# Moving four shares of y and their copy-out within the first quarter of each token group, in a fused attention and two-MLP kernel

## The chip, the cores and the metric

The kernel runs on one core of one Trainium2 chip. The metric is the device time of one execution, in microseconds (us), from launch to end, as the median of several runs. One further execution was recorded by the hardware profiler; all rows below come from it.

## What is computed

A pooled attention is followed by two MLPs without biases; the change touches the second MLP alone.

```python
def _moe2_ref(x, w_in, w_out):            # x: 4608 x 512
    h = x @ w_in                          # w_in: 512 x 2048
    relu6 = np.clip(h + 3.0, 0.0, 6.0)
    g = h * relu6 / 6.0
    return (g @ w_out).astype(np.float32) # w_out: 2048 x 512

def reference(...):
    attn_out = _attn_ref(q, k, v)         # softmax attention on keys and values pooled by 8
    x = attn_out, heads side by side      # 4608 x 512
    x = _moe_ref(x, w_in, w_out)          # as above, with g = h * sigmoid(h)
    return _moe2_ref(x, ...)
```

All of it is float32. A matrix product is made of three TensorE products of rounded parts (high by high, low by high, high by low), which is why most operands come in pairs such as `gh` and `gl`.

## The kernel before

**Staging.** The whole body stands in a manual schedule: each engine runs its instructions in the order in which the program issues them. A first stage (up to about 915 us of the span) does the attention and the first MLP and writes its result to the DRAM tensors `x1`. The second MLP is the loop at lines 851 to 918: `g` runs over 9 groups of 512 tokens, and inside it `d` runs over 4 quarters of the hidden units (512 units each, four blocks `f` of 128).

**A quarter.** The product with `w_in` is done by a seven-product block scheme: `product(bank, g, d, k)` (line 588) issues 12 matmuls of half width, and k is one of 0, 5, 4, 6, 3, 1, 2 in this order. Below they are P0, P5, P4, P6, P3, P1, P2. P0, P4 and P1 take turns on the two PSUM buffers of pool `ps_h`, the other four on the two of `ps_a`. A buffer is free again when VectorE (DVE) or ScalarE (ACT) has read it: `c1` is an ACT copy of P0 (line 878), and `add` (line 862) is a DVE addition that makes u2 = c1 + P5, then u3 = u2 + P6, u4 = u3 + P4, u2 = u2 + P4, later u3 + P3, c1 + P1 and u2 + P2. So P3 needs the buffer that the first addition frees, and P6 of the next quarter needs the one that the last addition frees.

**Activations.** `act_half` (line 609) is called four times in a quarter, for u4, u3, c1 and u2, in this order: an ACT relu (line 612), a DVE min-and-multiply (line 613), an ACT copy to the rounded high part `gh` (line 620), a DVE subtraction for the low part `gl` (line 621). Each of the four needs the one before. The first two calls fill `gh2` and `gl2`, from which blocks 1 and 3 of the quarter are read; the last two fill `gh1` and `gl1`, for blocks 0 and 2. ACT and DVE thus run one chain, and between two calls DVE does the next addition.

**Shares of y.** The product with `w_out` is added up over the 16 blocks of a group in four PSUM banks (pool `ps_y`, one buffer each). A share is one block's part: `y_mm` (line 508) issues 12 matmuls, three for each bank, with `gh` or `gl` as the weights. Shares wait in the list `todo`; `y_next` (line 844) issues the oldest. A quarter calls it four times: after P5, after the three additions behind P6, after the third `act_half`, and after the fourth. The shares of a quarter are thus issued in the next one; those of the last quarter (blocks 13, 15, 12, 14) come in the first quarter (d = 0) of the next group. Behind block 14 comes `y_out` (line 527): four copies out of the banks, two on ACT (line 532) and two on DVE (line 534), and four DMA issues on SyncE's queue (line 541). The next group's first share overwrites the banks, and so needs these copies.

**Other work of a quarter.** `passed(k)` issues on SyncE's queue the load of the next weights of product k (line 232). In the second quarter `load_x1` issues loads of the next group's x; in the third and fourth, `made` has GpSimd (POOL, lines 178 and 585) and ACT (line 584) make its seven block operands.

Of the kernel before, what the change touches and what calls it, by code (L numbers as in the profile page):

```python
# [25 lines left out]
def kernel(  # L26
# [54 lines left out]
    def shuffled(ap):  # L81
        return ap.rearrange("p (a n) -> p n a", a=2)
# [136 lines left out]
    def load_split(f):  # L219
        t = wts.tile([P, 2, DM], F32R, tag=f"o{f}", name="whl")  # L220
        nc.sync.dma_start(out=t.bitcast(F32), in_=w2[f])
        w_sl[1, f, 1] = (t[:, 0], t[:, 1])
# [6 lines left out]
    def load_factor(d, k):  # L229
        i = PASSING.index(k) if k in PASSING else 4 + 3 * d + STAYING.index(k)  # L230
        t = wts.tile([P, 2, 2, HW], F32R, tag=f"i{i}", name="wst")
        nc.sync.dma_start(out=t.bitcast(F32), in_=ws[d][k])
        w_st[d, k] = t
# [274 lines left out]
    def y_mm(layer, g, f):  # L508
        gh, gl = g_t.pop((layer, g, f))
        oh, ol = w_sl[layer, f, 1]  # L510
        if f == FIRST[layer]:
            y_ps[layer, g] = [
                ps_y.tile([P, 512], F32, tag=f"y{i}", name=f"y{i}") for i in range(4)
            ]
        for i, ps in enumerate(y_ps[layer, g]):
            sl = slice(i * P, (i + 1) * P)
            if layer == 0:
                prods = ((oh[:, sl], gh), (ol[:, sl], gh), (oh[:, sl], gl))
            else:
                prods = ((gh[:, sl], oh), (gh[:, sl], ol), (gl[:, sl], oh))  # L520
            for n, (a, b) in enumerate(prods):
                nc.tensor.matmul(  # L522
                    ps, a, shuffled(b), start=(f == FIRST[layer] and n == 0),
                    stop=(f == LAST[layer] and n == 2),
                )

    def y_out(layer, g):
        scale = 0.5 if layer == 0 else 1.0 / 6.0
        for i, ps in enumerate(y_ps.pop((layer, g))):
            o = p2.tile([P, 512], F32, tag="o", name="o", bufs=4)  # L530
            if i % 2 == 0:
                nc.scalar.activation(in_two(o), dealt(ps), AF.Copy, scale=scale)  # L532
            else:
                nc.vector.tensor_scalar(
                    out=in_two(o), in0=dealt(ps), scalar1=scale, scalar2=None, op0=ALU.mult
                )
            if layer == 0:
                dst = x1[g][i * P:(i + 1) * P, :]
            else:
                dst = out[g * GT + i * P:g * GT + (i + 1) * P, :]  # L540
            nc.sync.dma_start(out=dst, in_=o)
# [12 lines left out]
    def open_rest():  # L554

        four = p2.tile([P, 4, 2, GT], F32R, tag="x", name="xst")
        late["x"] += [four[:, i] for i in range(4)]

    def load_x1(g):

        for k in range(2):
            for n in range(2):
                r = late["pool"].tile([P, 2, HW], F32, tag="r", name="xr", bufs=4)
                rows = x1[g][k * HW:(k + 1) * HW, n * HW:(n + 1) * HW]
                nc.sync.dma_start(out=r, in_=rows.rearrange("(c p) t -> p c t", p=P))
                x_raw[k, n] = r.rearrange("p c t -> p (c t)")
# [3 lines left out]
    def make_x(g, i):  # L570

        k = MADE[i]
        b11, b12, b21, b22 = (x_raw[a, b] for a in range(2) for b in range(2))
        src = (b11, b11, b11, b12, b21, b21, b22)[i]
        if i == 1:
            combine(ALU.subtract, b11, b12, b11)
        elif i == 2:
            combine(ALU.subtract, b11, b22, b11)
        elif i == 3:
            combine(ALU.subtract, b12, b22, b12)  # L580
        elif i == 5:
            combine(ALU.subtract, b21, b21, b11)
        t = late["x"][(7 * g + i) % 9]
        nc.scalar.activation(t[:, 0], src, AF.Copy)  # L584
        nc.gpsimd.tensor_tensor(out=t[:, 1], in0=src, in1=t[:, 0].bitcast(F32), op=ALU.subtract)  # L585
        x_st[g, k] = t.rearrange("p a (c n) -> p a c n", c=2)

    def product(bank, g, d, k):

        pool, tag = bank  # L590
        ps = pool.tile([P, GT], F32, tag=tag, name=f"p{k}")
        w = w_st[d, k].rearrange("p j a (c f) -> p j a c f", f=P)
        x = x_st[g, k]
        for j in range(2):
            for n, (a, b) in enumerate(((0, 0), (1, 0), (0, 1))):
                for c in range(2):
                    nc.tensor.matmul(  # L597
                        ps[:, j * HW:(j + 1) * HW],
                        w[:, j, a, c, :],
                        shuffled(x[:, b, c, :]),  # L600
                        start=(j == 0 and n == 0 and c == 0),
                        stop=(j == 1 and n == 2 and c == 1),
                    )
        return ps

    def rows_of(name, bufs):
        return late["pool"].tile([P, 2, GT], F32R, tag=name, name=name, bufs=bufs)
# [44 lines left out]
    with tc.manual_schedule():  # L652
# [191 lines left out]
        def y_next():  # L844
            if todo:
                l, g, f = todo.pop(0)
                y_mm(l, g, f)
                if f == LAST[l]:
                    y_out(l, g)

        for g in range(NG):
            for d in range(NF // 4):
                more = g + 1 < NG
                nd = (d + 1) % (NF // 4)
                go = more or d + 1 < NF // 4
                c1 = p2.tile([P, GT], F32, tag="gh", name="c1")
                u2 = p2.tile([P, GT], F32, tag="gl", name="u2")
                u3 = late["pool"].tile([P, GT], F32, tag="u3", name="u3")
                u4 = late["pool"].tile([P, GT], F32, tag="u4", name="u4", bufs=1)

                def add(out, a, b):
                    nc.vector.tensor_tensor(out=out, in0=a, in1=b, op=ALU.add)  # L862

                def passed(k):
                    if go:
                        load_factor(nd, k)

                def made(*items):
                    for i in items:
                        make_x(g + 1, i)  # L870

                if g == 0 and d == 0:
                    open_rest()
                    make_x(0, 5)
                    make_x(0, 6)
                p1 = product((ps_h, "h"), g, d, 0)
                passed(0)
                nc.scalar.activation(c1, p1, AF.Copy)
                add(u2, c1, product((ps_a, "a"), g, d, 5))
                y_next()  # L880
                if g == 0 and d == 0:
                    load_split(NF - 1)
                if more and d == 1:
                    load_x1(g + 1)
                if more and d == 2:
                    made(0)
                p5 = product((ps_h, "h"), g, d, 4)
                passed(4)
                add(u3, u2, product((ps_a, "a"), g, d, 6))
                add(u4, u3, p5)  # L890
                add(u2, u2, p5)
                y_next()
                gh2, gl2 = rows_of("gh2", 1), rows_of("gl2", 1)
                act_half(u4, 1, gh2, gl2)
                if more and d == 2:
                    made(1)
                if more and d == 3:
                    made(2, 3)
                add(u3, u3, product((ps_a, "a"), g, d, 3))
                act_half(u3, 0, gh2, gl2)  # L900
                add(c1, c1, product((ps_h, "h"), g, d, 1))
                passed(1)
                gh1, gl1 = rows_of("gh1", 2), rows_of("gl1", 2)
                act_half(c1, 0, gh1, gl1)
                y_next()
                if more and d == 3:
                    made(4, 5)
                add(u2, u2, product((ps_a, "a"), g, d, 2))
                passed(2)
                act_half(u2, 1, gh1, gl1)  # L910
                y_next()
                if more and d == 3:
                    made(6)
                for f, gh, gl, j in ((1, gh2, gl2, 0), (3, gh2, gl2, 1), (0, gh1, gl1, 0), (2, gh1, gl1, 1)):
                    g_t[1, g, 4 * d + f] = (gh[:, j], gl[:, j])
                    todo.append((1, g, 4 * d + f))
# [50 lines left out]
```

## Time and profile before

| what | us |
|---|---|
| median of 3 runs (1687.97 to 1690.34) | 1690.16 |
| the profiled execution, device time | 1689.02 |
| its span, first to last instruction | 1687.2 |
| TensorE busy, share of the span | 95% |
| VectorE, ScalarE, GpSimd busy | 61%, 37%, 23% |

A row of the timeline gives start, duration, engine, line, operation, output and inputs, how many instructions are merged, and in brackets the idle time of the engine before it with what ended it. PE is TensorE's matmuls, PEld its weight loads. Times are us from the span's start. A row of the windows view gives for a stretch its length, the busy time of each engine with its instructions, the granted TensorE clock (1.00 is the full 2.4 GHz), the DMA share and the rate.

### The profile page before, as it was taken

The page shows a single profiled execution, that of the slowest core. Times are in us where ns is not written, and L with a number is a line of the kernel's source. Part 1 is how long each engine was busy: PE and PEld are TensorE (multiplying, and loading weights), DVE is VectorE, ACT ScalarE, POOL GpSimd, SP SyncE. Part 2 cuts the span into 40 slices and gives each one's busy share as a digit, 9 for nine tenths or more (in the row PEclk, how much of TensorE's full clock was granted, in tenths as well). Part 3 has the DMA queues.
Part 4 walks back from the last instruction along what each step waited for, and adds up shares of the span by engine and source line. Part 5 has one row for each costly group of instructions (what it writes and reads, how often), then busy time and mean ns, then how long its engine had stood idle before and what let it go on. Part 6 is the DMA issues. An engine that isn't in the chain of part 4 may idle for free.

```text
span 1687.2 us, 24141 instructions
## 1 busy us (share of the span) xinstructions
PE 1602.4 (95%) x9312; PEld 1419.0 (84%) x9312; DVE 1031.0 (61%) x1608; ACT 631.8 (37%) x1094; POOL 381.8 (23%) x377
## 2 busy tenths in 40 slices
PE   7787999999999999999999999999999999999999
PEld 6566888888888888888889898989898989898988
DVE  6999767677676777665423655555555555555554
ACT  5454433333343333333322433333333333333333
POOL 4755322222312132211021121212121212020200
PEclk9798999999999999999999999999999999999999
DMA  9251334344443445432356434343434343434341
GB/s 284 103 198 32 106 124 154 109 152 155 136 152 106 149 149 161 131 131 83 108 203 237 150 100 142 109 138 109 141 102 144 105 139 111 138 108 143 101 125 50
DMA packets 101330, 224.27 MB, mean 133 GB/s; under 512 B 10464, under 2 KB 35936, under 8 KB 101216
## 3 DMA queue, kind: packets, MB, share of 16 engines
q1 hardware_dynamic: 101216, 222.73, 41.3%
q8 instruction: 73, 1.20, 0.3%
q14 instruction: 41, 0.34, 0.1%
HBM read 169.74 MB, written 52.95 MB: 132 GB/s over the span
## 4 chain that ended last, share of the span: by engine, by line
PE 63%; DVE 16%; issue 9%; ACT 7%; DMA 3%; POOL 2%; SPq 0%; ACTq 0%; POOLq 0%; DVEq 0%
PE y L522 32%; PE hps L479 18%; PE p L597 10%; DVE t L613 3%; ACT t L612 3%; ACT gh L620 2%; DVE u L862 2%; DVE gl L621 2%; PE aps L340 1%; PE aps L444 1%; POOL xst L585 1%; DVE wmag L111 1%; DVE wmag L114 1%; POOL xr L178 1%; DVE gl L501 1%
## 5 line engine op out<-in xcount | busy, mean ns | idle before, releaser
L479 PE MATMUL hps<-x,whl 128*128 128x512 f32 x1728 | 400.2, 381 | 4.2 <-POOL whl L132 2.1
L522 PE MATMUL y<-whl,gh 128*128 128x512 f32 x1152 | 353.7, 389 | 30.4 <-ACT o L532 29.7
L597 PEld LDWEIGHTS p<-xst,wst 128*128 128x128 f32 x3024 | 359.0, 192 | 16.3 <-DVE u L862 9.2
L479 PEld LDWEIGHTS hps<-x,whl 128*128 128x128 f32 x1728 | 328.4, 190 | 52.3 <-POOL whl L132 2.5
L597 PE MATMUL p<-xst,wst 128*128 128x256 f32 x3024 | 361.6, 275 | 5.7 <-DVE u L862 5.7
L522 PE MATMUL y<-gh,whl 128*128 128x512 f32 x1152 | 359.2, 394 | 0.8 <-POOL whl L132 0.8
L522 PEld LDWEIGHTS y<-whl,gh 128*128 128x128 f32 x1152 | 213.4, 195 | 58.0 <-ACT o L532 31.3
L522 PEld LDWEIGHTS y<-gh,whl 128*128 128x128 f32 x1152 | 217.9, 194 | 37.6 <-issue 5.4
L522 PE MATMUL y<-gl,whl 128*128 128x512 f32 x576 | 224.6, 390 | 13.8 <-DVE gl L501 13.7
L585 POOL TENSOR_TENSOR xst<-xr,xst 128x512 fp32r<-128x512 f32 x63 | 83.0, 1317 | 659.5 <-ACT xst L584 653.6
L522 PE MATMUL y<-whl,gl 128*128 128x512 f32 x576 | 223.0, 387 | 0.1
L621 DVE TENSOR_TENSOR gl<-t,gh 128x512 fp32r<-128x512 f32 x144 | 113.6, 789 | 131.6 <-ACT gh L620 131.6
L492 DVE SCALAR_TENSOR_TENSOR t<-t,hps 128x512 f32<-128x512 f32 x144 | 97.7, 678 | 152.3 <-ACT t L491 151.4
L491 ACT ACTIVATE t<-hps 128x512 f32<-128x512 f32 x144 | 85.8, 596 | 275.6 <-PE hps L479 275.5
L501 DVE TENSOR_TENSOR gl<-t,gh 128x512 fp32r<-128x512 f32 x144 | 128.5, 893 | 90.5 <-ACT gh L500 90.5
L862 DVE TENSOR_TENSOR u<-u,p 128x512 f32<-128x512 f32 x180 | 120.2, 684 | 89.6 <-PE p L597 87.5
L612 ACT ACTIVATE t<-u,three 128x512 f32<-128x512 f32 x108 | 77.8, 720 | 251.0 <-DVE u L862 251.0
L174 POOL TENSOR_TENSOR hs<-hmag,hs 128x256 fp32r<-128x256 f32 x88 | 65.0, 743 | 470.6 <-ACT hs L173 415.0
L620 ACT ACTIVATE gh<-t 128x512 fp32r<-128x512 f32 x144 | 120.0, 833 | 127.6 <-DVE t L613 127.6
L500 ACT ACTIVATE gh<-t 128x512 fp32r<-128x512 f32 x144 | 90.7, 630 | 181.6 <-DVE t L492 180.9
L613 DVE SCALAR_TENSOR_TENSOR t<-t,u 128x512 f32<-128x512 f32 x108 | 91.0, 843 | 106.6 <-ACT t L612 106.6
L522 PEld LDWEIGHTS y<-gl,whl 128*128 128x128 f32 x576 | 112.0, 194 | 34.6 <-DVE gl L501 18.2
(86 smaller groups left out, 1360.1 us busy)
## 6 DMA issues: line engine op xcount, KB each, us to landing
wst<-ws SPq DMA_DIRECT2D x156, 512.0 KB
ws<-hs SPq DMA_DIRECT2D x56, 256.0 KB
bl<-bT SPq DMA_DIRECT2D x28, 384.0 KB
x<-o SPq DMA_DIRECT2D x36, 256.0 KB
xr<-x SPq DMA_DIRECT2D x36, 256.0 KB
out_dram<-o SPq DMA_DIRECT2D x36, 256.0 KB
wraw<-in_moe_w_in_dram SPq DMA_DIRECT2D x16, 512.0 KB
wraw<-in_moe_w_out_dram SPq DMA_DIRECT2D x16, 512.0 KB
```

Source lines behind the costliest of these rows:

```text
L479: nc.tensor.matmul(ps, w[:, c, :], shuffled(x[:, c, :]), start=(c == 0 and n == 0), stop=(c == NKC - 1 and n == 2),)
L492: nc.vector.scalar_tensor_tensor(out=t2, in0=t2, scalar=1.0, in1=h, op0=ALU.add, op1=ALU.mult)
L500: nc.scalar.activation(gh, t, AF.Copy)
L501: nc.vector.tensor_tensor(out=gl, in0=t, in1=gh.bitcast(F32), op=ALU.subtract)
L522: nc.tensor.matmul(ps, a, shuffled(b), start=(f == FIRST[layer] and n == 0), stop=(f == LAST[layer] and n == 2),)
L585: nc.gpsimd.tensor_tensor(out=t[:, 1], in0=src, in1=t[:, 0].bitcast(F32), op=ALU.subtract)
L597: nc.tensor.matmul(ps[:, j * HW:(j + 1) * HW], w[:, j, a, c, :], shuffled(x[:, b, c, :]), start=(j == 0 and n == 0 and c == 0), stop=(j == ...
L612: nc.scalar.activation(t, h, AF.Relu, bias=three)
L613: nc.vector.scalar_tensor_tensor(out=t, in0=t, scalar=6.0, in1=h, op0=ALU.min, op1=ALU.mult)
L620: nc.scalar.activation(oh, t3, AF.Copy)
L621: nc.vector.tensor_tensor(out=ol, in0=t3, in1=oh.bitcast(F32), op=ALU.subtract)
L862: nc.vector.tensor_tensor(out=out, in0=a, in1=b, op=ALU.add)
```

## The change

In the first quarter of each group but the first, two more calls of `y_next` are made: behind the ACT copy of P0, and behind P4. In exchange the two calls behind the third and the fourth `act_half` are left out when d = 0. In that quarter the order is then P0, block 13, P5, block 15, P4, block 12, P6, the three additions, block 14 with `y_out`, then the four `act_half` with P3, P1 and P2. The other quarters keep their order; in the first group the first quarter has one share only, which stays where it was.

```diff
+                early_y = d == 0 and g > 0
...
                 p1 = product((ps_h, "h"), g, d, 0)
                 passed(0)
                 nc.scalar.activation(c1, p1, AF.Copy)
+                if early_y:
+                    y_next()
                 add(u2, c1, product((ps_a, "a"), g, d, 5))
                 y_next()
...
                 p5 = product((ps_h, "h"), g, d, 4)
                 passed(4)
+                if early_y:
+                    y_next()
                 add(u3, u2, product((ps_a, "a"), g, d, 6))
                 add(u4, u3, p5)
                 add(u2, u2, p5)
                 y_next()
...
                 act_half(c1, 0, gh1, gl1)
-                y_next()
+                if d:
+                    y_next()
...
                 act_half(u2, 1, gh1, gl1)
-                y_next()
+                if d:
+                    y_next()
```

## Rows read from the trace of the kernel before

**Rows 1.** The page's list of engines: busy time, share of the span, instructions
```profile
PE 1602.4 (95%) x9312; PEld 1419.0 (84%) x9312; DVE 1031.0 (61%) x1608; ACT 631.8 (37%) x1094; POOL 381.8 (23%) x377
```

**Rows 2.** Waits from 915 us on: total us, times, longest
```profile
PE y L522 <- ACT o L532: 29.7, 8, 3.7
```

**Rows 3.** TensorE's timeline, where a share waits for a copy: first, second, last
```profile
1016.33 0.70 PE L522 MATMUL y<-whl,gh 128*128 128x512 f32 x2 [3.72 <-ACT o L532]
...
1101.91 0.94 PE L522 MATMUL y<-whl,gh 128*128 128x512 f32 x2 [3.71 <-ACT o L532]
...
1614.57 1.22 PE L522 MATMUL y<-whl,gh 128*128 128x512 f32 x2 [3.70 <-ACT o L532]
```

**Rows 4.** Windows: a quarter without a wait, a wait, the share after it
```profile
949.68:969.42 19.74, 19.74 (x133) 18.46 (x132) 11.93 (x17) 8.38 (x13) 5.17 (x4) 1.00 0.37 110
...
1098.20:1101.90 3.70, 0.01 (x1) 0.00 (x0) 2.13 (x4) 1.91 (x4) 0.00 (x0) 1.00 0.00 0
1101.90:1106.30 4.40, 4.39 (x13) 3.52 (x14) 1.99 (x4) 0.94 (x2) 0.00 (x0) 0.61 0.79 260
```

**Rows 5.** TensorE's timeline, first quarter of the third group; x24 is two products
```profile
1074.70 2.84 PE L597 MATMUL p<-xst,wst 128*128 128x256 f32 x24
1077.38 0.60 PE L522 MATMUL y<-whl,gh 128*128 128x512 f32 x2
...
1079.97 2.84 PE L597 MATMUL p<-xst,wst 128*128 128x256 f32 x24
...
1086.06 2.94 PE L597 MATMUL p<-xst,wst 128*128 128x256 f32 x24 [0.66 <-DVE u L862]
...
1106.29 2.84 PE L597 MATMUL p<-xst,wst 128*128 128x256 f32 x24
```

**Rows 6.** Timeline of ACT and DVE, from there into the next quarters
```profile
1084.32 0.85 DVE L621 TENSOR_TENSOR gl<-t,gh 128x512 fp32r<-128x512 f32 x1 [0.96 <-ACT gh L620]
...
1086.11 2.01 DVE L862 TENSOR_TENSOR u<-u,p 128x512 f32<-128x512 f32 x3
...
1088.37 0.69 DVE L613 SCALAR_TENSOR_TENSOR t<-t,u 128x512 f32<-128x512 f32 x1 [0.25 <-ACT t L612]
...
1090.84 0.68 DVE L862 TENSOR_TENSOR u<-u,p 128x512 f32<-128x512 f32 x1
...
1094.01 0.85 DVE L621 TENSOR_TENSOR gl<-t,gh 128x512 fp32r<-128x512 f32 x1 [0.95 <-ACT gh L620]
...
1098.46 0.68 DVE L862 TENSOR_TENSOR u<-u,p 128x512 f32<-128x512 f32 x1
...
1109.17 2.00 DVE L862 TENSOR_TENSOR u<-u,p 128x512 f32<-128x512 f32 x3 [5.28 <-PE p L597]
...
1125.29 0.67 DVE L862 TENSOR_TENSOR u<-c,p 128x512 f32<-128x512 f32 x1
```

**Rows 7.** Timeline where a share waits for its own gh and gl, and that window
```profile
931.24 0.79 DVE L621 TENSOR_TENSOR gl<-t,gh 128x512 fp32r<-128x512 f32 x1 [0.72 <-ACT gh L620]
...
932.08 0.48 PE L522 MATMUL y<-whl,gl 128*128 128x512 f32 x1
...
934.35 1.50 PE L597 MATMUL p<-xst,wst 128*128 128x256 f32 x12
...
930.00:933.00 3.00, 2.25 (x12) 1.58 (x11) 1.90 (x3) 0.94 (x2) 0.00 (x0) 1.00 0.94 331
```

**Rows 8.** Timeline at the program's end: last share and last copy
```profile
1680.49 0.59 PE L522 MATMUL y<-whl,gh 128*128 128x512 f32 x2
...
1683.28 0.69 DVE L534 TENSOR_SCALAR o<-y 128x512 f32<-128x512 f32 x1 [0.60 <-PE y L522]
```

**Rows 9.** A stall in the first stage, and the window behind it
```profile
155.30 0.76 PE L340 MATMUL aps<-kbd,qT 128*128 128x144 f32 x4 [1.91 <-DVE x L461]
...
157.00:160.20 3.20, 3.20 (x9) 2.48 (x9) 3.15 (x5) 0.28 (x1) 2.42 (x3) 0.51 0.01 2
```

**Rows 10.** SyncE's queue: the next weights of P0 behind the four copies out
```profile
1104.15 0.39 SPq L232 DMA_DIRECT2D wst<-ws  x1
```

## The prediction, made before the changed kernel was run

> **What bounds the kernel now.** I read the page's list of engines first: TensorE is busy for 95% of the span, no other engine for more than 61% [rows 1]. So time is to be had only where TensorE stands still or runs slowly. The list of waits, cut to the second MLP, says where: TensorE waits 29.7 us for the ACT copies of y_out, in eight waits of at most 3.7 us [rows 2]. TensorE's timeline puts one of them at every change of group, always at the first share of the new group [rows 3]. The windows then show that such a wait costs twice. The granted clock is 1.00 during the wait, but 0.61 in the 4.40 us behind it [rows 4], a mix of its two levels, 1.2 and 2.4 GHz. The share of y there lasts from 1101.91 to 1106.29, 4.38 us [rows 3, 5], where an undisturbed one lasts 1079.97 - 1077.38 = 2.59 us [rows 5]: 1.79 us more.
>
> A group lasts (1614.57 - 1016.33) / 7 = 85.46 us [rows 3]; four quarters without a wait would last 4 x 19.74 = 78.96 us [rows 4]. The difference of 6.5 us closes: the wait with its start-up (about 3.9), the slow share (1.8), and a third, smaller wait, 0.66 us idle before P3, whose PSUM buffer the addition u2 = c1 + P5 frees late [rows 5], with its start-up some 0.9.
>
> Why are the copies late? They stand behind the four act_half in the queues of ACT and DVE, and that chain lags behind TensorE in the first quarter: P0 and P5 start at 1074.70 [rows 5], but the last low part of the quarter before is ready at 1084.32 + 0.85 = 1085.17, and the three additions come at 1086.11 [rows 6].
>
> **The change, part by part.** No work is added or removed. I lay out TensorE's new first quarter with 1.34 us for a product (half of 1077.38 - 1074.70) and 2.59 us for a share [rows 5], from the same start, 1074.70.
>
> (a) Shares 13 and 15, earlier. P0 ends at 1076.04, share 13 at 1078.63, P5 at 1079.97, share 15 at 1082.56, P4 at 1083.90. Blocks 13 and 15 were read from 1077.38 on in the kernel before too, from parts filled before the last two act_half; I price this at nothing. If it failed, the cost would be the delay of those parts, one for one.
>
> (b) Share 12, earlier, is a new wait. It would start at 1083.90, but its low part is ready at 1085.17 only [rows 6], the high part 0.9 us before. The nearest rows are those of the second quarter of the first group, where a share caught up with its own activation: low part ready at 931.24 + 0.79 = 932.03, its first matmul at 932.08, end of the share 934.35 - 932.08 = 2.27 us later [rows 7]. So share 12 ends at 1085.17 + 0.05 + 2.27 = 1087.49, 1.00 us late. On TensorE everything is queued behind it: P6, then the three additions. Bounds: 0.8, if the weight loads were hidden, to 1.5, if the chain is half a microsecond slower. Of those loads the Trainium skill says that TensorE pulls them ahead of matmuls in flight (TensorE: Matmul & The Clock Gate, section "Step-by-step: what each phase is for"); by that rule 10 matmuls would take 10 x 2.59 / 12 = 2.16 us and the wait 0.89, some 0.9 us less over eight changes of group. The row has 2.27, so the late weights themselves are not pulled ahead.
>
> (c) P6 ends at 1088.83, share 14 runs to 1091.42. The additions read P6, and start 0.2 us after its end (at 1109.17 behind products that end at 1106.29 + 2.68 = 1108.97 [rows 5, 6]): 1089.03, ending at 1091.04.
>
> (d) y_out, now ahead of the activations. Each copy waits for its own bank only: at the program's end the last copy starts 2.79 us after the share's first matmul and lasts 0.69 [rows 8]. Here that is 1088.83 + 2.79 = 1091.62, and 1092.31 for its end. Behind it on DVE stands the min-and-multiply of the first act_half, which was at 1088.37 [rows 6] and comes at about 1092.35. The whole chain of the quarter is thus late by 4.0 us: 2.9 because P6 comes later, 1.1 because of the copies. Bounds: 2.9, if the copies fit into the relu's time, to 4.6, if a copy waits for the whole share and is paid on both engines. I take 4.0, since DVE runs in order and the rows at the program's end show this order of share and copy.
>
> (e) P3, P1, P2 and the next quarter's P0 and P5 follow without a share between: 1091.42 + 5 x 1.34 = 1098.12. The buffers are free: the latest, that of P5, is freed by u3 + P3, which ended at 1090.84 + 0.68 = 1091.52 before [rows 6] and at 1095.5 now, while P5 starts at 1096.78. y's banks have been free since 1092.3, so **the wait for the copies is gone**. Next late is the low part of act_half(u3): 1094.01 + 0.85 = 1094.86 before [rows 6], 1098.86 now. By the price of (b) the share ends at 1098.86 + 0.05 + 2.27 = 1101.18, 0.46 late.
>
> (f) P4 ends at 1102.52. P6 needs the buffer that u2 + P2 frees, before at 1098.46 + 0.68 = 1099.14 [rows 6], now at 1103.14: TensorE waits 0.67, and with the 0.1 that products took longer behind a wait (2.94 for 2.84) [rows 5] P6 ends at 1104.63. Before, it ended at 1108.97. **The gain is 4.34 us at a change of group.** The old wait before P3 is in it, since the first addition is now long done.
>
> (g) Does the chain catch up? Its next three additions come when the last act_half, c1 and u2 are through, at about 1106.7; before they came at 1109.17 after DVE had waited 5.28 us for TensorE [rows 6]. From there to the end of the next u2 = c1 + P5 it took 1125.96 - 1109.17 = 16.8 us [rows 6], so 1123.5 now, while TensorE ends that P6 at 1104.63 + 19.74 = 1124.37. DVE waits again, with 0.9 us to spare, and from there the group runs as before.
>
> (h) Queues. SyncE's four issues of y_out move ahead of the loads for P1 and P2; they are through at about 1092.5, before P1 ends at 1094.1, so they hold nothing. Their weights have 14.5 us to the next P1. Before, the load for P0 was issued at 1104.15, behind the copies out [rows 10], for a product at 1106.29 + 14.5 = 1120.8, 16.6 us later, with no wait for it. GpSimd has no work in this quarter.
>
> The sum: 8 x 4.34 = 34.7 us. The profiled execution took 1689.02 us, so it would take 1654.3; the median of the runs is 1.14 above it, which gives 1655.4.
>
> **The rivals.**
> Small waits vanish: only (b) stays. The group is then 78.96 + 1.0, a gain of 5.5, 44 us: 1646. It needs a chain delay below about 3.3; (d) speaks against it.
>
> The clock falls once at each change nevertheless. Where TensorE stood still for 1.91 us in the first stage, the 3.2 us behind it ran at 0.51 [rows 9]; where a share waited for its own parts, and TensorE was busy for 2.25 of 3.00 us, the window kept 1.00 [rows 7]. The wait of (b) is the second case, of about the same size. One fall costs 1.79, the gain is 2.55, 20 us: 1670.
>
> The chain becomes the bound: the margin of 0.9 in (g) is wrong, the lag passes through the quarters, and share 12 waits longer in each group. It must be late by 4.3 beyond that margin, and beyond a further slack of some 2 us in the later quarters, to eat the gain; then the time is about 1690.
>
> The other side: the clock falls at each of the three new waits, (b), (e) and (f). Three falls cost 5.37, more than 4.34, and the kernel is 1.03 x 8 = 8 us slower: 1698. It decides from the third fall on; that the window of rows 7 kept its clock speaks against it.
>
> That the change does not do what it says would need y's banks to be held by something else; the waits list only the copies [rows 2], so this gets no case of its own.
>
> **How the numbers follow.** The forecast has 0.73, the small-waits case 0.09, the single fall 0.10, the bound chain 0.04, the three falls 0.04. A measurement can tell about 0.2%, 3.4 us, from no change. Faster: 0.73 + 0.09 + 0.10 = 0.92; within: 0.04; slower: 0.04. The bounds of (b) and (d) allow some 0.6 us per change to either side, 5 us in all; the range reaches on to the small-waits case and the single fall, 1646 to 1670.
>
> **What would show it.** After: no wait of a share for the copies; four shares and P0, P5, P4, P6 alternating in the first quarter; a share waiting about 1 us in two pieces for its activation, then about 0.4, and P6 0.7 for an addition; the first share of a group at 2.6 to 3.0 us, clock 1.00; groups of about 81.1 us. It is wrong if the clock is under 1.00 behind any of these waits, if a share waits for gl by 2 us or more, or if DVE no longer waits for P6 in the later quarters.

## The result and the profile after

The changed kernel takes 1642.63 us (median; 1641.74 to 1642.79) against 1689.23 us before (four runs; the median of 1690.16 stood on three of them): a ratio of 0.972, 95% interval 0.971 to 0.974, 46.6 us less. The forecast was 1655.4 with a range from 1646 to 1670: the sign held, and the wait for the copies is gone as forecast, but two of the new waits that were priced did not come, and the time lies 3.4 us below the range.

TensorE's share of busy time rose from 95% [rows 1] to 97%. The list of waits from 915 us on, of the changed kernel, no longer has the copies of y_out on TensorE's side [rows 2]; the additions make it wait for 4.5 us in all:

```profile
PE p L597 <- DVE u L864: 4.5, 9, 0.6
PE y L522 <- ACT gh L620: 0.6, 1, 0.6
```

Eight of the nine waits of the first line are at the changes of group; the ninth, and the one of the second line, are in the first group, which the change leaves alone. TensorE's timeline of the changed kernel, first and last of the eight:

```profile
1014.40 0.82 PE L597 MATMUL p<-xst,wst 128*128 128x256 f32 x5 [0.51 <-DVE u L864]
...
1572.65 1.60 PE L597 MATMUL p<-xst,wst 128*128 128x256 f32 x12 [0.48 <-DVE u L864]
```

A group now lasts (1572.65 - 1014.40) / 7 = 79.75 us, where it lasted 85.46 [rows 3]. That is 0.79 above the 78.96 of four quarters without a wait [rows 4], and 8 x 5.71 = 45.7 us are the saving to within 1 us.

Here is a first quarter on TensorE after the change (it answers to rows 5; x60 is P3, P1, P2 and the next quarter's P0 and P5):

```profile
1067.14 1.50 PE L597 MATMUL p<-xst,wst 128*128 128x256 f32 x12
...
1075.00 1.50 PE L597 MATMUL p<-xst,wst 128*128 128x256 f32 x12
1076.34 0.60 PE L522 MATMUL y<-whl,gh 128*128 128x512 f32 x2
...
1078.93 1.50 PE L597 MATMUL p<-xst,wst 128*128 128x256 f32 x12
1080.27 0.60 PE L522 MATMUL y<-whl,gh 128*128 128x512 f32 x2
...
1082.86 6.86 PE L597 MATMUL p<-xst,wst 128*128 128x256 f32 x60
...
1089.56 0.60 PE L522 MATMUL y<-whl,gh 128*128 128x512 f32 x2
1089.99 0.38 PE L522 MATMUL y<-whl,gl 128*128 128x512 f32 x1
...
1092.15 1.50 PE L597 MATMUL p<-xst,wst 128*128 128x256 f32 x12
...
1094.16 1.60 PE L597 MATMUL p<-xst,wst 128*128 128x256 f32 x12 [0.51 <-DVE u L864]
...
1095.60 0.60 PE L522 MATMUL y<-whl,gh 128*128 128x512 f32 x2
```

From P0 at 1067.14 to the new group's share at 1089.56 no row carries an idle time. The one wait left stands before P6 of the second quarter. P6 ends at 1095.60, 28.46 us after P0; before it ended at 1108.97, 34.27 us after P0 at 1074.70 [rows 5]. That is 5.8 us for this change of group, where 4.34 were forecast.

The same stretch on ACT and DVE (it answers to rows 6):

```profile
1076.79 0.83 DVE L621 TENSOR_TENSOR gl<-t,gh 128x512 fp32r<-128x512 f32 x1 [0.89 <-ACT gh L620]
...
1080.47 2.01 DVE L864 TENSOR_TENSOR u<-u,p 128x512 f32<-128x512 f32 x3 [1.99 <-PE p L597]
...
1081.12 0.60 ACT L532 ACTIVATE o<-y 128x512 f32<-128x512 f32 x1 [3.36 <-PE y L522]
...
1082.39 1.36 DVE L534 TENSOR_SCALAR o<-y 128x512 f32<-128x512 f32 x2
...
1083.67 0.68 DVE L613 SCALAR_TENSOR_TENSOR t<-t,u 128x512 f32<-128x512 f32 x1
1084.38 0.80 ACT L620 ACTIVATE gh<-t 128x512 fp32r<-128x512 f32 x1 [0.77 <-DVE t L613]
...
1088.98 0.75 DVE L621 TENSOR_TENSOR gl<-t,gh 128x512 fp32r<-128x512 f32 x1 [0.88 <-ACT gh L620]
...
1093.43 0.68 DVE L864 TENSOR_TENSOR u<-u,p 128x512 f32<-128x512 f32 x1
...
1115.56 2.01 DVE L864 TENSOR_TENSOR u<-u,p 128x512 f32<-128x512 f32 x3 [0.48 <-PE p L597]
```

The first row is the puzzle: this low part is ready at 1077.62, and share 12, which reads it, started at 1076.34 and did not wait. The copies now come between the additions and the activations, as the change wants it. The last row is the third quarter, where DVE waits for TensorE again: the lag is caught up.

### The profile page after: what moved, and what is told of

It reads as the page before. It is cut to its first block, busy times and chain, and to the rows that moved or that the text cites. A ratio compares the mean times of both kernels' runs of the same rounds, so it can differ in the third digit from the quotient of the medians.

```text
span 1639.9 us, 24118 instructions
## 1 busy us (share of the span) xinstructions
PE 1585.7 (97%) x9312; PEld 1409.8 (86%) x9312; DVE 1029.6 (63%) x1608; ACT 632.9 (39%) x1094; POOL 383.5 (23%) x377
## 4 chain that ended last, share of the span: by engine, by line
PE 77%; DVE 13%; DMA 3%; ACT 3%; issue 2%; SPq 0%; ACTq 0%; DVEq 0%
PE y L522 40%; PE hps L479 19%; PE p L597 16%; PE aps L340 1%; PE aps L444 1%; DVE u L864 1%; ACT gh L620 1%; DVE wmag L111 1%; DVE gl L621 1%; DVE gl L501 1%; DVE wmag L114 1%; DVE t L613 1%; DVE kbd L271 1%; DVE wmag L121 1%; ACT t L612 1%
## 5 line engine op out<-in xcount | busy, mean ns | idle before, releaser
L522 PE MATMUL y<-whl,gh 128*128 128x512 f32 x1152 | 343.1, 379 | 0.6 <-ACT gh L620 0.6
L522 PEld LDWEIGHTS y<-whl,gh 128*128 128x128 f32 x1152 | 207.3, 190 | 24.2 <-ACT gh L620 0.8
L522 PE MATMUL y<-whl,gl 128*128 128x512 f32 x576 | 218.4, 379 | 0.1
```

What stands on the lines that cost most here:

```text
L522: nc.tensor.matmul(ps, a, shuffled(b), start=(f == FIRST[layer] and n == 0), stop=(f == LAST[layer] and n == 2),)
```

## The experiments

**1. Share 12 with its banks turned.** Why did the new wait of step (b) not come? The code holds an answer: `act_half` fills one half of the tokens, and the share's bank i reads tokens 128 i to 128 i + 127. Of `gh1` the third call (c1) fills the first half and the fourth (u2) the second. Banks 0 and 1 thus need only the earlier call, and bank 2 comes 1.3 us into the share. If that is the reason, turning the banks must bring the wait back.

```diff
-        for i, ps in enumerate(y_ps[layer, g]):
+        for i in order:                 # (0, 1, 2, 3) but for share 12
+            ps = y_ps[layer, g][i]
...
                 passed(4)
                 if early_y:
-                    y_next()
+                    y_next((2, 3, 0, 1))
```

> The changed kernel, but the early share of block 12 goes through its banks in the order 2, 3, 0, 1. Theory (the share did not wait because its first six matmuls, for banks 0 and 1, read only the token half that the third act_half made, and the late half is read 1.3 us later): now its first matmuls need the part that is ready 10.48 us after P0's start, while the share can start 9.20 us after it; a wait of about 1.0 us in each of 8 changes of group comes back, passed on to P6 and the additions, 8 us: about 1650.6 against 1642.6. Rival (the parts of block 12 are ready in time for another reason, and the order of the banks does not matter): 1642 to 1643, no new wait.

Measured: 1649.45 us, 6.8 more than the changed kernel (ratio to before 0.977, 0.976 to 0.979). TensorE's timeline of it, with P4 first and P6 last:

```profile
1075.55 1.50 PE L598 MATMUL p<-xst,wst 128*128 128x256 f32 x12
1077.28 0.70 PE L523 MATMUL y<-whl,gh 128*128 128x512 f32 x2 [0.23 <-ACT gh L621]
1078.10 0.48 PE L523 MATMUL y<-whl,gl 128*128 128x512 f32 x1
...
1080.37 1.50 PE L598 MATMUL p<-xst,wst 128*128 128x256 f32 x12
```

The share waits for the high part, then after two matmuls for the low part, and P6 starts 0.89 us later than 1075.55 + 1.34 + 2.59 = 1079.48. That is the wait that step (b) priced at 1.00: its price was nearly right, for a half of the tokens that the share does not read first. The share ends 1080.37 - 1078.10 = 2.27 us after the first matmul with the low part, as in [rows 7]. The rival falls. The window behind the wait, and P6 of the second quarter at the first and the last change of group:

```profile
1078.10:1082.50 4.40, 4.40 (x26) 4.05 (x27) 1.28 (x2) 0.13 (x1) 1.08 (x1) 1.00 0.32 114
```

```profile
1014.95 1.60 PE L598 MATMUL p<-xst,wst 128*128 128x256 f32 x12 [0.51 <-DVE u L865]
...
1579.53 1.60 PE L598 MATMUL p<-xst,wst 128*128 128x256 f32 x12 [0.51 <-DVE u L865]
```

The granted clock stayed at 1.00. A group lasts (1579.53 - 1014.95) / 7 = 80.65 us, 0.90 more than in the changed kernel. (The kernel before took 1687.67 us beside experiments 1 to 4, 1.6 less than beside the changed kernel; differences of a few us between the two sets are therefore read from the groups too.)

**2. The early shares without the early copies.** y_out goes back behind the fourth activation; the shares stay where the change puts them. (`y_next` gets an argument: with a false one it issues the share without y_out.)

```diff
                 add(u2, u2, p5)
-                y_next()                # with y_out
+                y_next(not early_y)     # without y_out
...
                 act_half(u2, 1, gh1, gl1)
+                if early_y:
+                    y_out(1, g - 1)
```

> The changed kernel with its early shares, but y_out behind the fourth act_half as in the kernel before. Theory (the gain is that of the copies; the early shares only make them possible): the first copy comes about 28.1 us after P0's start, the new group's share could start at 22.4 and waits some 6.3 us, with a low clock behind; P6 of the second quarter ends at about 35.8 after P0's start, against 34.3 in the kernel before: 12 us slower than that, about 1700. Rival (placing the shares between the first products is the gain, the copies matter little): 1642 to 1650.

Measured: 1706.08 us, ratio to before 1.011 (1.009 to 1.012). It is slower than the kernel before, as the theory has it and by 6 us more. One of its waits in TensorE's timeline, and the window behind it:

```profile
1104.66 1.22 PE L522 MATMUL y<-whl,gh 128*128 128x512 f32 x2 [6.06 <-ACT o L532]
...
1109.94 3.17 PE L597 MATMUL p<-xst,wst 128*128 128x256 f32 x24
```

```profile
1104.70:1109.10 4.40, 4.40 (x11) 3.50 (x12) 1.95 (x4) 0.88 (x2) 0.00 (x0) 0.50 0.81 264
```

The wait grew from 3.7 [rows 3] to 6.06 us: TensorE is there 0.9 us sooner after P0, as it no longer waits before P3, and the copies come 1.4 us later after P0, because P6, which the additions read, now stands behind the shares. The granted clock behind it was 0.50 for all of the window, where it was 0.61 [rows 4], and the share took 1109.94 - 1104.66 = 5.28 us, where it took 4.38; these 0.9 us, less the 0.2 by which the wait is shorter than forecast, make up in 8 changes most of the 6 us by which 1700 was too low. Moving the shares by itself is a loss; the gain is that of the copies, which the early shares make possible.

**3. The wait filled.** How much of the old loss was the clock? In the kernel before, 28 unread matmuls keep TensorE busy during most of the wait.

```diff
                 add(u2, c1, product((ps_a, "a"), g, d, 5))
+                if d == 1 and g > 0:
+                    fill(g, d, 28)      # 28 matmuls of 256 columns into one ps_h buffer
                 y_next()
```

> The kernel before, with 28 further matmuls of 256 columns (some 3.1 us, result unread) on TensorE ahead of each new group's first share, where TensorE waited 3.7 us for the copies. Theory (1.79 us of the loss at a change of group is the low clock behind the wait): the share still starts when the copies are done, but at clock 1.00 and in 2.6 us; 8 x 1.8 = 14 us less than before, about 1675. Rival (the slow share is slow for another reason, such as the loads and copies out that run then): 1688 to 1690, the share still at 4.4 us.

Measured: 1677.86 us, ratio to before 0.994 (0.993 to 0.995), 9.8 us less by doing more. Its timeline on TensorE and the window of the share:

```profile
1095.28 3.29 PE L610 MATMUL fill<-xst,wst 128*128 128x256 f32 x28
...
1099.31 0.70 PE L522 MATMUL y<-whl,gh 128*128 128x512 f32 x2 [0.75 <-ACT o L532]
...
1102.20 2.84 PE L597 MATMUL p<-xst,wst 128*128 128x256 f32 x24
```

```profile
1099.30:1102.00 2.70, 2.69 (x12) 2.12 (x13) 1.99 (x4) 0.93 (x2) 0.00 (x0) 1.00 0.65 240
```

The share takes 1102.20 - 1099.31 = 2.89 us at clock 1.00, for 4.38 at 0.61 [rows 3 to 5], while the loads and copies out run beside it as before (240 GB/s): the rival falls. Of the 1.79 that the prediction put down to the clock, 1.49 came back at the full clock. The other 0.3 shows at the full clock: the share's first matmuls are slower behind the short wait that is left, and it waits for bank 1's copy on DVE (the matmuls for bank 1 start 0.84 us after those for bank 0, not 0.65). In the slow share of the kernel before it did not wait for it: bank 1 came 1.16 us after bank 0, and the later banks 1.28 apart. A group of this kernel lasts 84.19 us, 1.27 less than before; the copies also came 0.17 later after the products, and this is most of what is missing to 1.49. The forecast of 1675 was 3 us too low, in the main for these two reasons.

**4. The copies woven into the activations.** The changed kernel's last wait was put down to the delay of the chain by the copies. Here they stand where ACT and DVE wait for each other anyway. (`y_out` gets the banks that it copies as an argument.)

```diff
-    def act_half(h, half, gh, gl):
+    def act_half(h, half, gh, gl, between=None):
...                                      # relu on ACT, multiplication on DVE
+        if between:
+            between()
...                                      # high part on ACT, low part on DVE
                 add(u2, u2, p5)
-                y_next()
+                y_next(not early_y)     # without y_out
-                act_half(u4, 1, gh2, gl2)
+                act_half(u4, 1, gh2, gl2, early_y and (lambda: y_out(1, g - 1, (0, 1))))
...
-                act_half(u3, 0, gh2, gl2)
+                act_half(u3, 0, gh2, gl2, early_y and (lambda: y_out(1, g - 1, (2, 3))))
```

> The changed kernel, but the four copies of y_out stand between the multiplication and the high-part copy of the first two act_half (banks 0 and 1 in the first, 2 and 3 in the second), where ACT and DVE wait for each other anyway. Theory (the one wait left, 0.5 us before P6 of the second quarter, is the chain's delay by the copies, 0.9 us): the wait goes, about 0.6 us in each of 8 changes: about 1637.7. Rival (the copies lengthen the chain wherever they stand, or the wait has another cause): 1641 to 1643.

Measured: 1636.00 us, ratio to before 0.969 (0.968 to 0.971), 6.6 us below the changed kernel, where 4.9 were expected; it is the fastest version of this study. The windows from 1000 to 1600 us, of the changed kernel and of this one:

```profile
1000.00:1600.00 600.00, 596.04 (x3982) 555.24 (x3982) 337.88 (x472) 237.74 (x338) 100.61 (x77) 1.00 0.42 132
```

```profile
1000.00:1600.00 600.00, 600.00 (x4021) 560.90 (x4020) 341.87 (x478) 239.64 (x341) 100.42 (x77) 1.00 0.41 134
```

TensorE has no idle time left there, and does 39 matmuls more in the same 600 us. The five products of the first and the last change of group give the length of a group:

```profile
1002.84 6.86 PE L598 MATMUL p<-xst,wst 128*128 128x256 f32 x60
...
1555.56 6.86 PE L598 MATMUL p<-xst,wst 128*128 128x256 f32 x60
```

It is (1555.56 - 1002.84) / 7 = 78.96 us, that of four quarters without a wait [rows 4], and 0.79 less than in the changed kernel: the wait before P6 with its start-up, 6.3 us over eight changes. The timeline of this kernel shows P0 and then the copies in the gaps:

```profile
1066.08 1.50 PE L598 MATMUL p<-xst,wst 128*128 128x256 f32 x12
...
1081.67 0.69 DVE L614 SCALAR_TENSOR_TENSOR t<-t,u 128x512 f32<-128x512 f32 x1 [0.25 <-ACT t L613]
...
1082.28 0.69 DVE L535 TENSOR_SCALAR o<-y 128x512 f32<-128x512 f32 x1
1082.39 0.80 ACT L623 ACTIVATE gh<-t 128x512 fp32r<-128x512 f32 x1 [0.28 <-DVE t L614]
1083.23 0.75 DVE L624 TENSOR_TENSOR gl<-t,gh 128x512 fp32r<-128x512 f32 x1 [0.27 <-ACT gh L623]
```

The copy on DVE fills the time in which DVE waited for the high part; its wait there is 0.27 instead of 0.9.

**5. The shares all behind the additions.** Without the two new calls between products: three shares in a row with y_out, where the change has one. The changed kernel ran again beside it.

```diff
                 nc.scalar.activation(c1, p1, AF.Copy)
-                if early_y:
-                    y_next()
...
                 passed(4)
-                if early_y:
-                    y_next()
...
                 add(u2, u2, p5)
                 y_next()
+                if early_y:
+                    y_next()
+                    y_next()
```

Expected of the changed kernel run again:

> The changed kernel once more, on the chip of the two runs beside it, so that they can be compared with it: 1642 to 1643.

Expected of this kernel:

> The changed kernel without its two new calls between the products: the first quarter runs P0, P5, block 13, P4, P6, the three additions, and then blocks 15, 12 and 14 in one go with y_out, ahead of the activations as in the changed kernel. Theory (what counts is that the four shares and four products end before the activations, 15.7 us after P0's start in any order; the first act_half then waits for the last two copies alone): the same time as the changed kernel within 2 us, 1641 to 1645, with the same single wait of 0.5 us before P6 of the second quarter; the additions run 2 us earlier and bring nothing. Rival 1 (P6 coming 1.9 us late is what delays the chain, as the prediction had it): the wait before P6 goes, 5 us less, about 1637. Rival 2 (the alternation of products and shares matters, for the PSUM buffers): some us more, 1650.

Measured: 1642.68 us, beside 1642.99 for the changed kernel: no difference. DVE and TensorE in this kernel:

```profile
1067.77 2.84 PE L597 MATMUL p<-xst,wst 128*128 128x256 f32 x24
...
1079.18 2.01 DVE L864 TENSOR_TENSOR u<-u,p 128x512 f32<-128x512 f32 x3
...
1083.69 0.69 DVE L534 TENSOR_SCALAR o<-y 128x512 f32<-128x512 f32 x1 [0.60 <-PE y L522]
...
1084.30 0.68 DVE L613 SCALAR_TENSOR_TENSOR t<-t,u 128x512 f32<-128x512 f32 x1
...
1094.79 1.60 PE L597 MATMUL p<-xst,wst 128*128 128x256 f32 x12 [0.51 <-DVE u L864]
```

P0 is at 1067.77 here, so the additions come 11.4 us after it, 1.9 earlier than in the changed kernel. The first multiplication comes 16.53 us after it, in both kernels: it stands behind the last copy, which here waits for share 14. So between these two orders the places of the first three shares do not matter, and to bring P6 and the additions forward gains nothing by itself: the chain then waits until share 14 is copied out. In the changed kernel the two paths end together: its two DVE copies follow the additions without idle time (the row at 1082.39).

**6. A wide fill.** The chain ran faster after the change than its rows of before said. To see whether TensorE's work beside it is the cause, 17 unread matmuls of 512 columns that stream w_out fill the old wait.

```diff
+                if d == 1 and g > 0:
+                    fill(g, d, 17)      # 17 matmuls of 512 columns of w_out
```

> The kernel before, with 17 unread matmuls of 512 columns that stream w_out (3.7 us) where the kernel before waited for the copies. It asks why the chain of the changed kernel ran faster than priced. Theory (the ACT copy to the high part and the DVE subtraction take longer while TensorE streams shares than while it runs products: 0.88 and 0.85 us for 0.80 and 0.75): the high-part copy of the fourth act_half, 0.66 us beside an idle TensorE, takes 0.85 to 0.90 beside these matmuls. Rival (the durations follow the chain's own position or the operands' places, not TensorE): 0.66 to 0.75.

Measured in one execution: 1679.99 us. The high-part copy of the fourth activation, first in the timeline of the kernel before, beside an idle TensorE, then in this one:

```profile
1100.71 0.66 ACT L620 ACTIVATE gh<-t 128x512 fp32r<-128x512 f32 x1 [0.76 <-DVE t L613]
```

```profile
1096.13 3.83 PE L610 MATMUL fill<-whl,wst 128*128 128x512 f32 x17
...
1098.94 0.88 ACT L629 ACTIVATE gh<-t 128x512 fp32r<-128x512 f32 x1 [0.76 <-DVE t L622]
```

It takes 0.88 us beside these matmuls, for 0.66. In experiment 3 the fill of 256 columns ended at 1095.28 + 3.29 = 1098.57, and the same copy stood beside it for most of its time:

```profile
1098.03 0.74 ACT L629 ACTIVATE gh<-t 128x512 fp32r<-128x512 f32 x1 [0.76 <-DVE t L622]
```

The theory holds for the copy; the subtraction behind it was not tested, as the fill had all but ended by then. Which of the two, the width or the operand, makes the difference is not told apart.

## Why the prediction was wrong in size

**What held.** The bound, the eight waits, their two prices (but for the 0.3 us of experiment 3) and the smaller third wait were read rightly: groups shrank by 5.71 of the 6.5 us named as the loss. Step (a) cost nothing. The clock stayed at 1.00: no fall came behind the new wait (the window of the changed kernel in experiment 4), and none behind the 0.89 us of experiment 1, whose cost is that of the wait alone. Step (f) named the right wait: P6 of the second quarter waits 1094.16 - (1092.15 + 1.34) = 0.67 us for the addition of that step. That this is the price to the hundredth is luck: TensorE reached that point 1.47 us earlier after P0 than forecast, and so did the addition, 1.1 of it by step (d) and the rest by a chain that ran faster than any step had it. Steps (g) and (h) held too: DVE waits for TensorE again in the third quarter, 0.48 us, where 0.9 were forecast, and no wait of TensorE for a load shows.

**Step (b) failed.** It priced a new wait of 1.00 us for share 12; there was none. The step took a share as one reader of a whole `gh` and `gl`. The code shows that a share goes through the tokens in four slices, and that the fourth activation fills the second half alone; the 1.3 us of the first two banks cover what the share would have waited. Experiment 1 shows it by making the share read the late half first. The row from which (b) was priced [rows 7] was of another kind: there the half that is read first is the one made last, because for `gh2` the second of its two calls fills the first half. Its bounds, 0.8 to 1.5, did not hold zero, and this left the time out of the range. The step also read from 2.27 us, for the 2.16 of ten matmuls in a stream, that late weights are not pulled ahead; the rows do not show that it is the late weights: P6, which waits for a buffer alone, is 0.10 longer behind its wait as well (1.60 for 1.50).

**Step (d) followed it.** The first multiplication came 1083.67 - 1067.14 = 16.53 us after P0, where it came at 13.67 before: the chain is late by 2.86 us, not 4.0. Of the 1.1 us of difference 1.0 is (b)'s, which was handed on through P6 and share 14. The step's split of the rest, 1.9 for P6 and 1.1 for the copies, fits experiment 4: with the copies out of the way the first multiplication comes 1081.67 - 1066.08 = 15.59 us after P0, 1.92 late, so that the copies add 0.94. But the two are not a sum of which either part can be had alone: in experiment 5 the additions are 1.9 us earlier and the delay is the same.

**Step (e) failed by itself.** It had the new group's share wait 0.46 us for the low part of the second activation. That part is ready at 1089.73, and the matmul that needs it came at 1089.99. This does not follow from (b): the 1.0 us that (b) had too much delayed the chain and the share alike. The term that failed is the length of the chain, taken from rows of before: from the first multiplication to this low part it took 6.06 us, where it was 1094.86 - 1088.37 = 6.49 [rows 6]. With 6.49 the part would be ready at 1090.16, too late. Its high-part copies took 0.80 to 0.81 us and its subtractions 0.75, where they took 0.88 to 0.89 and 0.85; beside them TensorE ran products, where it had run shares. That this is the reason is shown for the copies, so far as experiment 6 goes; for the subtractions it is read from the rows alone.

Together (b) and (e) are 1.46 us of a change of group, the difference between 4.34 and 5.8, and 11.7 of the 12.8 us by which the forecast missed; 0.9 more is the median before, 1690.16 in the forecast and 1689.23 in the end. The rival "small waits vanish" had the right size of change, and its condition, a delay of the chain below 3.3 us, was met; but it kept the wrong wait, (b), and what stayed was (f). Experiment 4 shows what (f) is worth, and that the wait goes when the copies are moved.

## What to carry to other kernels

When a moved step reads a buffer that is filled in parts, ask which slice its first instruction reads and which instruction fills that slice; a wait priced for the whole buffer can be hidden by the step's own first half. A copy-out that frees a resource for the critical engine can stand where the engines that do it wait for each other, and need not delay their chain: here putting it ahead of the chain gave 47 us, and weaving it in a further 6.6. A stall of the critical engine that also brings its clock down costs more than its length, here 1.5 us on top of 3.7; filling the stall with unread work shows how much of the loss is the clock's.

## What the runs showed of the hardware

The ScalarE copy to the rounded high part (128x512) took 0.66 us with TensorE idle, 0.80 with 256-column products beside it and 0.88 with 512-column shares; the VectorE subtraction took 0.69, 0.75 and 0.85 in such rows, without an experiment of its own. A price for such an instruction, taken from a row, holds for the TensorE work that stood beside that row.
